# The last 512 tokens of a second layer by Strassen's seven products instead of eight

## The chip, the cores and the metric

The kernel runs on one core of a Trainium2 chip. The metric is the device time of one launch in microseconds, taken as the median of several runs. The engines are TensorE (PE, matmuls; PEld is its weight load), VectorE (DVE), ScalarE (ACT), GpSimd (POOL) and SyncE (SP), which only issues transfers. SBUF is the on-chip memory, PSUM the accumulators that TensorE writes.

## The reference

Eight batches of attention with RMS-normalised queries and keys (12 heads, 448 tokens, 64 channels) give 3584 tokens of 768 channels. They go through two layers with a tanh-GELU between:

```python
q_n, k_n = rmsnorm(q, g_q), rmsnorm(k, g_k)
attn = softmax(q_n @ k_n.T / sqrt(64))
x = (attn @ v) as (3584, 768)
h = x @ w_in                      # 768 -> 2048
g = gelu_tanh(h)
out = g @ w_out                   # 2048 -> 768, float32
```

## The kernel before

The work goes batch by batch. `attention(b)` computes the scores, exponentials and products of batch b, and between them TensorE runs the second layer of earlier batches, in steps whose order is a string written out by hand. Behind each attention comes the first layer of that batch (`mm1_turn`, line 537), whose result ScalarE passes through the GELU (line 543) into `g`.

`g` is one SBUF tile of 128 partitions, 16 slices f of d_ff, and 2 x 448 tokens: two batches side by side. `wout` holds the second layer's weights, 128 partitions, the same 16 slices f, and 768 columns. Both are bf16. A second-layer result for 128 tokens is a sum over the 16 slices f. Two batches make seven such token tiles. Those that `attention` takes are computed with 64 x 64 tiles of the array (`quartered`, line 495); the ones that are left after the last batch, tiles 3 to 6 of the last pair, 512 tokens, are computed by `final` with the full array (`whole`, line 463): for each token tile two halves of HD = 384 columns, each 16 matmuls. The last half of the last tile is cut in two pieces of 192 columns. Each piece is copied from PSUM to an SBUF tile `osb` by ScalarE (line 704) or VectorE (line 706) and stored by `store` (line 456), two transfers of 64 rows each. Those go to SP's queue; the last ones are shared between SP and ScalarE.

PSUM tiles come from `pair`, which hands out four tiles in turn (t_100, t_101, t_892 and t_893 in the program's names).

In the first layer of the last batch, eight GELUs each fill two slices f of `g` (896 elements per partition). The list `m1` holds functions that are issued at given steps f of that layer; for the last batch it is empty. The order on every engine is that of the code; a wait is put before an instruction for the regions that it reads and writes.

Other names: `kT` holds the transposed keys, `vb` two tiles of values, and tiles with tag `ex` hold exponentials; nothing reads them behind the last attention. `sqp` is a pool for squares of queries and keys.

Of the kernel before, what the change touches and what calls it, by code (L numbers as in the profile page):

```python
# [8 lines left out]
F32 = mybir.dt.float32  # L9
BF16 = mybir.dt.bfloat16  # L10
# [7 lines left out]
def kernel(  # L18
# [11 lines left out]
    nc = tc.nc  # L30
    B, H, S, D = q.shape
    assert (B, H, S, D) == (8, 12, 448, 64)
    d_model = H * D
# [4 lines left out]
    P = 128  # L38
    R = 64
    NT = S // R  # L40
    NCH = H // 4
    HP = H // 2
    nf = d_ff // 128
    HD = d_model // 2
# [6 lines left out]
    sqp = ctx.enter_context(tc.tile_pool(name="sqp", bufs=2))  # L51
# [4 lines left out]
    exq = ctx.enter_context(tc.tile_pool(name="exq", bufs=2))  # L56
    xp = ctx.enter_context(tc.tile_pool(name="xp", bufs=2))
    gp = ctx.enter_context(tc.tile_pool(name="gp", bufs=1))
    op = ctx.enter_context(tc.tile_pool(name="op", bufs=3))
# [3 lines left out]
    start = ctx.enter_context(ExitStack())  # L63
# [6 lines left out]
    def pair(name):  # L70
        rounds.append(rounds.pop(0))
        return rounds[-1]
# [35 lines left out]
    wout = wts.tile([128, nf, d_model], BF16)  # L108
    vb = [wts.tile([P, HP, NT, D], BF16, name=f"vb{i}") for i in range(2)]
    ones = consts.tile([P, D], BF16)  # L110

    kT = consts.tile([128, NCH, NT, 2, R], BF16)
    raws, sqs, sss, rinvs, nrms = {}, {}, {}, {}, {}
    qT, xT = {}, {}
    g = gp.tile([128, nf, 2 * S], BF16, tag="g", name="g")
# [54 lines left out]
    def total(b, c, n, hs=both, ts=slice(0, NT)):  # L170
        if b not in sss:
            sss[b] = smp.tile([P, NCH, 2, 2, NT], F32, tag="ss", name="ss")
        nc.vector.reduce_sum(  # L173
            sss[b][:, seat(b, c), "qk".index(n), hs, ts], squares(b, c, n, hs, ts), axis=AX.X
        )
# [44 lines left out]
    def rsqrt_newton(b):  # L220


        rinvs[b] = smp.tile([P, NCH, 2, 2, NT], F32, tag="rinv", name="rinv")
        cs, flat = slice(0, NCH - 1), "p c n a t -> p (c n a t)"
        y, ms = rinvs[b][:, cs].rearrange(flat), sss[b][:, cs].rearrange(flat)
        t = smp.tile([P, NCH * 4 * NT], F32, tag="lg", name="lg")[:, :(NCH - 1) * 4 * NT]
        nc.vector.tensor_scalar(ms, ms, 1.0 / D, 1e-6, op0=ALU.mult, op1=ALU.add)
        nc.vector.tensor_scalar(
            y.bitcast(I32), ms.bitcast(I32), -0.5, float(0x5F3759DF), op0=ALU.mult, op1=ALU.add
        )  # L230
        for i in range(3):
            nc.vector.tensor_mul(t, y, y)
            nc.vector.scalar_tensor_tensor(t, t, -0.5, ms, op0=ALU.mult, op1=ALU.mult)
            if i < 2:
                nc.vector.scalar_tensor_tensor(y, t, 1.5, y, op0=ALU.add, op1=ALU.mult)

        m = 2 * NT
        for js, dst in ((slice(m, None), y[:, m:]), (slice(0, m), place(b, 0)[:, :m])):
            nc.vector.scalar_tensor_tensor(
                dst, t[:, js], 1.5, y[:, js], op0=ALU.add, op1=ALU.mult  # L240
            )

    def rsqrt_last(b, c=slice(NCH - 1, NCH)):

        flat, m = "p c n a t -> p (c n a t)", (c.stop - c.start) * 4 * NT
        y, ms = rinvs[b][:, c].rearrange(flat), sss[b][:, c].rearrange(flat)
        dst, z, u = y, None, ms
        if not steady():
            z, u = oall[0][:, S:S + m], oall[0][:, S + m:S + 2 * m]
            dst = place(b, 1)  # L250
        t = smp.tile([P, NCH * 4 * NT], F32, tag="lg", name="lg")[:, :m]
        nc.vector.tensor_scalar(u, ms, 1.0 / D, 1e-6, op0=ALU.mult, op1=ALU.add)
        nc.vector.tensor_scalar(
            y.bitcast(I32), u.bitcast(I32), -0.5, float(0x5F3759DF), op0=ALU.mult, op1=ALU.add
        )
        for i in range(3):
            if z is not None:
                nc.vector.tensor_copy(z, y)
            half = t if z is None else z
            nc.vector.tensor_mul(t, y if z is None else z, y)  # L260
            nc.vector.scalar_tensor_tensor(half, t, -0.5, u, op0=ALU.mult, op1=ALU.mult)
            nc.vector.scalar_tensor_tensor(
                y if i < 2 else dst, half, 1.5, y, op0=ALU.add, op1=ALU.mult
            )
# [8 lines left out]
    def normed(b, c, n, eng, ts=slice(0, NT)):  # L273
        if (n, b, c) not in nrms:
            nrms[n, b, c] = nrmp.tile([P, NT, 2, D], BF16, tag=f"nrm{n}", name=f"nrm{n}")
        m = ts.stop - ts.start
        root = rinvs[b][:, seat(b, c), "qk".index(n)] if eng is nc.gpsimd else roots[n, b, c]
        eng.tensor_mul(  # L278
            nrms[n, b, c][:, ts].rearrange("p t a d -> p a t d"),
            raws[n, b, c][:, :, ts],  # L280
            root[:, :, ts].to_broadcast([P, 2, m, D]),
        )
# [28 lines left out]
    def trans(b, c, eng=nc.vector):  # L311
        for n in "qk":
            turn(b, c, n)
            put(b, c, n, eng=eng)
# [9 lines left out]
    def gain(b, c):  # L324
        nc.vector.tensor_scalar(kT[:, c], kT[:, c], gcol[:, 0:1], None, op0=ALU.mult)
# [121 lines left out]
    osbs = {}  # L447

    def osb_of(i):
        osbs[i] = op.tile([128, d_model], F32, tag="osb", name="osb")  # L450

    def store(b, i, lo=0, hi=d_model, engs=(nc.sync, nc.sync)):
        for j, eng in enumerate(engs):
            col = i * 128 + j * R
            r = ((b // 2) * 2 + col // S) * R
            eng.dma_start(
                out_v[col % S // R, r:r + R, lo:hi], osbs[i][j * R:(j + 1) * R, lo:hi]
            )

    def whole(i, o, lo, hi):  # L460

        for f in range(nf):
            nc.tensor.matmul(  # L463
                o, g[:, f, i * 128:(i + 1) * 128], wout[:, f, lo:hi],
                start=(f == 0), stop=(f == nf - 1),
            )
# [117 lines left out]
    def attention(b, side, extra, ends):  # L584
# [57 lines left out]
        def go_on():  # L642
            for queue, eng in ((vector, nc.vector), (scalar, nc.scalar), (vector, nc.vector)):
                while queue and made.issuperset(needs(*queue[0])):
                    run(*queue.pop(0), eng)
# [41 lines left out]
        made.add(("p", 1))  # L687
        go_on()

    def final(b):  # L690

        last = 2 * S // 128 - 1
        for i in range(last - 3, last + 1):
            osb_of(i)
            for half in range(2):
                parts = [(half * HD, (half + 1) * HD)]
                if half and i == last:
                    parts = [(HD, HD + HD // 2), (HD + HD // 2, d_model)]
                for lo, hi in parts:
                    po = pair("o")[:, 0, :hi - lo]  # L700
                    whole(i, po, lo, hi)
                    end = hi == d_model
                    if half == 0 or i == last and not end:
                        nc.scalar.copy(osbs[i][:, lo:hi], po)
                    else:
                        nc.vector.tensor_copy(osbs[i][:, lo:hi], po)  # L706
                    if i == last and half:
                        store(b, i, lo if end else 0, hi, (nc.sync, nc.scalar))
            if i < last:
                store(b, i)  # L710

    def first_attention(side, mid):

# [25 lines left out]
    def plan(*entries):  # L739
        steps = {}  # L740
        for slot, *fns in entries:
            steps.setdefault(slot, []).extend(fns)
        return steps
# [185 lines left out]
    def normed_both(b, c, eng):  # L929
        for n in "qk":  # L930
            normed(b, c, n, eng)

    for b in range(B):
        m1, side, extra, ends = [], [], [], []
        if b == 0:

            m1 = [(0, lambda: total(1, 0, "k"),
                   lambda: total(1, 2, "q"), lambda: total(1, 2, "k"),
                   lambda: rsqrt_newton(1), lambda: normed_both(1, 2, nc.gpsimd),
                   lambda: normed(1, 0, "k", nc.gpsimd)),  # L940
                  (2, lambda: total(1, 1, "q"), lambda: total(1, 1, "k"),
                   lambda: normed(1, 0, "q", nc.vector), lambda: rsqrt_last(1),
                   lambda: normed_both(1, 1, nc.vector)),
                  (6, lambda: trans(1, 0, nc.scalar)),
                  (7, lambda: trans(1, 1))]
# [45 lines left out]
                extra.append(("first", lambda n=n: total(b + 2, 2, n)))  # L991
        if 0 < b and b + 1 < B:
            extra.append(("first", lambda: gain(b + 1, 2)))
        m1 = plan(*m1)
        for f in range(nf // 2 if b == 0 else nf):
            i, part = f // 4 * 2, f % 4
# [24 lines left out]
        if b + 1 == B:  # L1021
            final(b)
            break
# [44 lines left out]
```

## Time and profile before

| what | value |
|---|---|
| runs | 390.85, 390.27, 390.86 us; median 390.85 |
| profiled execution | span 389.1 us from the first to the last instruction; the page gives no other time of it |
| TensorE busy | 381.8 us (98%) |
| VectorE busy | 242.0 us (62%) |
| ScalarE busy | 278.2 us (71%) |
| GpSimd busy | 126.1 us (32%) |
| granted TensorE clock | 1.000 |
| last first layer on TensorE | 346.31 to 364.47 us |
| last stage on TensorE | 364.47 to 385.43 us |

Times in the profile count from the start of the span. A group of instructions reads: line, engine, operation, output and inputs by name, partitions x elements and type, count, busy us, mean ns of one, and the idle time of the engine just before it with what ended it. Matmuls are pipelined, so the length of one is more than the step from one to the next. A few per cent of the matmul records can be missing.

### The profile page before, as it was taken

What the parts mean: (1) busy time and instruction counts of PE and PEld (TensorE: products, weight loads), DVE (VectorE), ACT (ScalarE), POOL (GpSimd) and SP (SyncE); (2) the same over time, 40 slices, a digit from 0 to 9 for tenths busy, and PEclk for the clock granted to TensorE, in tenths of its full rate; (3) what the DMA queues carried; (4) which work ended last, traced back from release to release, by engine and by line L of the source; (5) the groups of instructions that cost most, each with busy time, mean ns of one, the idle gap of its engine ahead of it and who ended that gap; (6) DMA issues with size and microseconds to landing.
All of it is one profiled execution on the core that took longest, in us unless ns stands there. A gap on an engine that the chain in (4) does not pass through costs nothing.

```text
span 389.1 us, 17513 instructions
## 1 busy us (share of the span) xinstructions
PE 381.8 (98%) x8044; PEld 296.3 (76%) x8044; DVE 242.0 (62%) x367; ACT 278.2 (71%) x351; POOL 126.1 (32%) x109
## 2 busy tenths in 40 slices
PE   8899999999999999999999999999999999999996
PEld 5465586679987788877888788877888778887664
DVE  5998939985896359836589257953688304980010
ACT  6995589777994689757995589946897449944300
POOL 5996504448005440093103740063400900000000
PEclk9999999999999999999999999999999999999999
DMA  7999999979914992269722995169622721120033
GB/s 258 326 232 210 210 222 239 260 175 192 209 44 106 256 197 60 76 154 257 133 64 65 189 253 103 47 115 241 110 68 61 121 48 42 44 65 4 2 81 83
DMA packets 64446, 54.68 MB, mean 141 GB/s; under 512 B 37620, under 2 KB 60020, under 8 KB 64372
## 3 DMA queue, kind: packets, MB, share of 16 engines
q1 hardware_dynamic: 53936, 41.33, 44.0%
q0 software_dynamic: 10128, 11.80, 18.3%
q8 instruction: 63, 1.03, 1.1%
q10 hardware_dynamic: 308, 0.43, 0.3%
q14 instruction: 11, 0.09, 0.1%
HBM read 45.61 MB, written 11.01 MB: 146 GB/s over the span
## 4 chain that ended last, share of the span: by engine, by line
PE 92%; ACT 4%; DMA 1%; POOL 1%; SPq 0%; DVE 0%; issue 0%; DVEq 0%
PE t L537 33%; PE t L495 32%; PE t L387 9%; PE t L335 7%; PE t L463 5%; PE t L556 4%; ACT ex L343 4%; DMA rawq<-in_q_dram 1%; POOL g L164 1%; PE h L436 1%; PE o L387 0%; PE tp L296 0%; SPq L750 0%; DVE ss L173 0%; PE os L387 0%
## 5 line engine op out<-in xcount | busy, mean ns | idle before, releaser
L343 ACT ACTIVATE ex<-t,shift 128x896 bf16<-128x896 f32 x168 | 156.2, 1012 | 2.6 <-PE t L335 2.1
L495 PE MATMUL t<-wout,g 64*64 64x384 bf16 (+1 forms) x3456 | 152.0, 305 | 0.0
L495 PEld LDWEIGHTS <-g 64*64 64x64 bf16 x3456 | 115.3, 107 | 17.7 <-issue 0.2
L537 PE MATMUL t<-xT,win 64*64 64x448 bf16 x2688 | 128.7, 349 | 0.0
L537 PEld LDWEIGHTS <-win 64*64 64x64 bf16 x2688 | 97.8, 107 | 29.4
L543 ACT ACTIVATE g<-t 128x896 bf16<-128x896 f32 x56 | 50.5, 915 | 56.8 <-PE t L537 56.7
L173 DVE TENSOR_REDUCE ss<-sq 128x14 f32<-128x896 f32 (+3 forms) x45 | 44.3, 999 | 48.7 <-ACT sq L162 46.4
L335 PE MATMUL t<-qT,kT 64*64 64x448 bf16 x672 | 59.7, 352 | 1.9 <-ACT ex L343 0.6
L800 POOL COPY mark<-es 1x1 bf16<-1x1 bf16 x7 | 1.2, 177 | 134.9 <-DVE es L362 126.6
L278 POOL TENSOR_TENSOR nrmq<-rawq,rinv 128x896 bf16<-128x896 f32 (+1 forms) x21 | 34.8, 1659 | 18.8 <-ACT rinv L205 8.4
L355 DVE TENSOR_TENSOR es<-ex 128x1792 bf16<-128x1792 bf16 x21 | 22.2, 1059 | 29.5 <-ACT ex L343 29.5
L278 POOL TENSOR_TENSOR nrmk<-rawk,rinv 128x896 bf16<-128x896 f32 (+1 forms) x21 | 34.6, 1647 | 0.0
L387 PE MATMUL t<-ex,vb 64*64 64x448 bf16 x588 | 32.4, 350 | 0.2 <-issue 0.2
L335 PEld LDWEIGHTS <-kT 64*64 64x64 bf16 x672 | 26.1, 106 | 8.1 <-DVE kT L305 2.0
L397 DVE STREAM_TRANSPOSE st<-t 128x448 f32<-128x448 f32 x42 | 24.8, 628 | 9.2 <-PE t L387 9.2
L387 PEld LDWEIGHTS <-vb 64*64 64x64 bf16 x672 | 23.2, 107 | 8.3 <-issue 1.8
L409 DVE STREAM_TRANSPOSE rb<-rc 128x896 f32<-128x896 f32 (+1 forms) x25 | 26.7, 1068 | 0.3
L706 DVE COPY osb<-t 128x384 f32<-128x384 f32 (+1 forms) x4 | 2.0, 508 | 35.2 <-PE t L463 35.2
L422 DVE TENSOR_TENSOR xT<-t,rb 128x896 bf16<-128x896 f32 x21 | 22.8, 1087 | 0.9
L513 ACT COPY osb<-t 128x768 f32<-128x768 f32 (+1 forms) x18 | 12.6, 700 | 14.0 <-PE t L495 14.0
L358 DVE TENSOR_TENSOR es<-es,ex 128x1792 bf16<-128x1792 bf16 x21 | 22.3, 1062 | 0.0
L164 POOL TENSOR_TENSOR sq<-rawq 128x896 f32<-128x896 f32 (+1 forms) x9 | 13.6, 1510 | 24.1 <-DVE ss L173 17.4
(102 smaller groups left out, 318.4 us busy)
## 6 DMA issues: line engine op xcount, KB each, us to landing
rawq<-in_q_dram SPq DMA_DIRECT2D x22, 448.0 KB, 5.0
rawk<-in_k_dram SPq DMA_DIRECT2D x22, 448.0 KB, 6.3
out_dram<-osb SPq DMA_DIRECT2D x42, 192.0 KB, 2.7
vb<-in_v_dram POOLq DMA_DIRECT2D x6, 672.0 KB, 7.6
win<-in_moe_w_in_dram POOLq DMA_DIRECT2D x8, 384.0 KB, 11.1
wout<-in_moe_w_out_dram POOLq DMA_DIRECT2D x3, 768.0 KB, 17.6
out_dram<-osb SPq DMA_DIRECT2D x24, 96.0 KB, 2.5
vb<-in_v_dram POOLq DMA_DIRECT2D x2, 448.0 KB, 16.2
```

What stands on the lines that cost most here:

```text
L173: nc.vector.reduce_sum(sss[b][:, seat(b, c), "qk".index(n), hs, ts], squares(b, c, n, hs, ts), axis=AX.X)
L278: eng.tensor_mul(nrms[n, b, c][:, ts].rearrange("p t a d -> p a t d"), raws[n, b, c][:, :, ts], root[:, :, ts].to_broadcast([P, 2, m, D]),)
L335: nc.tensor.matmul(sc[r * R:(r + 1) * R, a, :S], kT[rs, c, t, r], qT[b][rs, c, :, r], start=True, stop=True,)
L343: nc.scalar.activation(exs[b, c][:, t], scs.pop((b, c, t))[:, :, :S], AF.Exp, scale=scale, bias=shift)
L358: nc.vector.tensor_add(es, es, ex[:, 4:6])
L387: nc.tensor.matmul(o[r][a * D:(a + 1) * D], vb[b % 2][rs, 2 * c + a, i] if what else ones[rs], es[i][rs, a], start=(i == 0), stop=(i == n ...
L397: nc.vector.transpose(st[:, r].rearrange("p a b -> p (a b)"), o[r])
L409: nc.vector.transpose(oas["rb"][:, rs].rearrange("p r s -> p (r s)"), rc.to_broadcast([128, (rs.stop - rs.start) * m, 32]),)
L422: nc.vector.tensor_mul(xT[b][:, 2 * c:2 * c + 2], oas["o", c, 1][:, :, :S], oas["rb"])
L495: mm = nc.tensor.matmul(o[a * R:(a + 1) * R, bank, :hi - lo], g[rs, f, at:at + R], wout[rs, f, lo:hi], start=(n == 0), stop=(n == len(step ...
L537: mm = nc.tensor.matmul(h[a * R:(a + 1) * R, j, :S], win[rs, c, at:at + R], xT[b][rs, c], start=begin and c == cs[0], stop=end and c == cs ...
L543: nc.scalar.activation(g[:, 2 * i:2 * i + 2, (b % 2) * S:(b % 2 + 1) * S], h[:, :, :S], AF.Gelu_apprx_tanh,)
```

## The change

The 512 tokens are taken as two groups of 256 (A1 and A2), the 16 slices f as eight pairs, and the 768 columns as two halves. That makes each operand a 2 x 2 block matrix: A11 is the first group at the even slices, A12 at the odd ones, A21 and A22 the same for the second group; B11 and B12 are the column halves of `wout` at the even slices, B21 and B22 at the odd ones. Each of the eight block products of before is a sum over 8 slices; the changed `final` makes seven (Winograd's form of Strassen's method), each for two token tiles of 128.

Four sums of weight blocks and four of token blocks are needed first. VectorE makes them: `weight_sum` and `token_sums` are put into the list `m1` of the last first layer, and the last quarter of the token sums stands at the head of `final`. The sums go to tiles with tag `ex`, to `kT`, to both tiles of `vb`, and in place to `wout` (B12) and `g` (A21). Products 1 and 2 need no sums and come first. Every product but the first of each tile is evicted by a VectorE add of PSUM and an `osb` tile; product 5 is added twice. The stores are of half width (384 columns), and the last of 192.

```diff
+    def token_sums(js):
+        a11, a21 = g4[:, js, 0, late1], g4[:, js, 0, late2]
+        a12, a22 = g4[:, js, 1, late1], g4[:, js, 1, late2]
+        nc.vector.tensor_sub(sa[3][:, js], a21, a11)
+        nc.vector.tensor_add(sa[2][:, js], sa[3][:, js], a22)
+        nc.vector.tensor_add(a21, a21, a22)
+        nc.vector.tensor_sub(sa[4][:, js], a12, sa[2][:, js])
...
+    def weight_sum(i):
+        x, y = {3: (b12, b22), 2: (b11, sw[3]), 4: (b21, sw[2]), 1: (b12, b11)}[i]
+        nc.vector.tensor_sub(sw[i], x, y)
...
     def final(b):
-        for i in range(last - 3, last + 1):
...
-                    whole(i, po, lo, hi)
...
+        token_sums(slice(NJ - 2, NJ))
...
+        def product(i, t, lo=0, hi=HD):
+            o = pair("o")[:, 0, :hi - lo]
+            for j in range(NJ):
+                lhs, rhs = operands(i, j, t)
+                nc.tensor.matmul(o, lhs, rhs[:, lo:hi], start=(j == 0), stop=(j == NJ - 1))
+            return o
...
+        for t in range(2):
+            c1, c2 = tiles[t]
+            nc.scalar.copy(c2[:, first], product(1, t))
+            add(c1[:, first], product(2, t), c2[:, first])
+            put_out(t, 0, first)
+        for t in range(2):
+            c1, c2 = tiles[t]
+            add(c1[:, last], product(6, t), c2[:, first])
+            add(c2[:, first], product(7, t), c1[:, last])
+            p5 = product(5, t)
+            add(c2[:, last], p5, c2[:, first])
+            add(c1[:, last], p5, c1[:, last])
+            put_out(t, 1, last)
+            add(c2[:, first], product(4, t), c2[:, first])
+            put_out(t, 1, first)
+            if t == 0:
+                add(c1[:, last], product(3, t), c1[:, last])
+                put_out(t, 0, last)
+                continue
+            for lo in (0, HD // 2):
+                cols = slice(HD + lo, HD + lo + HD // 2)
+                add(c1[:, cols], product(3, t, lo, lo + HD // 2), c1[:, cols])
+                put_out(t, 0, cols, (nc.sync, nc.scalar))
...
+        if b + 1 == B:
+            m1.append((4, sums_homes))
+            m1 += [(f, lambda i=i: weight_sum(i)) for f, i in ((4, 3), (6, 2), (8, 4), (10, 1))]
+            m1 += [(f, lambda js=js: token_sums(js))
+                   for f, js in ((7, slice(0, 4)), (11, slice(4, 6)))]
```

Here NJ is 8, g4 and w4 are views of `g` and `wout` with the slices f as pairs, late1 and late2 are the two groups of 256 tokens, sw and sa are the sums, and c1 and c2 the `osb` tiles of the first and the second group. `operands` gives for products 1 and 2 blocks of `g` and `wout`, for 3 sa[4] and B22, for 4 A22 and sw[4], for 5, 6 and 7 a sum of each.

More of the change, by code (lines that the diff above doesn't have):

```diff
@@ L688, in attention @@
         go_on()
-    def final(b):
-        last = 2 * S // 128 - 1
-        for i in range(last - 3, last + 1):
[L694 to L700, printed above, removed]
-                    whole(i, po, lo, hi)
[L702 to L710, printed above, removed]
+    NJ = nf // 2
@@ new lines, with sums_homes, home @@
+    g4 = g.rearrange("p (j w) s -> p j w s", w=2)
+    w4 = wout.rearrange("p (j w) d -> p j w d", w=2)
+    TH = 2 * 128
+    late1, late2 = slice(2 * S - 2 * TH, 2 * S - TH), slice(2 * S - TH, 2 * S)
+    sw, sa = {}, {}
+    def sums_homes():
+        two = exq.tile([P, 2 * NJ, HD], BF16, tag="ex", name="tw")
+        one = exq.tile([P, NJ, HD], BF16, tag="ex", name="tw")
+        sw.update({3: two[:, :NJ], 2: two[:, NJ:], 4: one})
+        sw[1] = w4[:, :, 0, HD:]
+        def home(t):
+            return t[:, :NJ * TH].rearrange("p (j s) -> p j s", j=NJ)
+        sa[1] = g4[:, :, 0, late2]
+        sa[2] = home(kT.rearrange("p c t r s -> p (c t r s)"))
+        sa[3] = home(vb[0].rearrange("p h t d -> p (h t d)"))
+        sa[4] = home(vb[1].rearrange("p h t d -> p (h t d)"))
@@ new lines, in weight_sum @@
+    def weight_sum(i):
+        b11, b12 = w4[:, :, 0, :HD], w4[:, :, 0, HD:]
+        b21, b22 = w4[:, :, 1, :HD], w4[:, :, 1, HD:]
+        x, y = {3: (b12, b22), 2: (b11, sw[3]), 4: (b21, sw[2]), 1: (b12, b11)}[i]
[7 more added lines that the diff above has]
+        nc.vector.tensor_sub(sa[4][:, js], a12, sa[2][:, js])
@@ new lines, in final, with operands, put_out @@
+    def final(b):
+        token_sums(slice(NJ - 2, NJ))
+        tiles = [[op.tile([128, d_model], F32, tag="osb", name="osb") for _ in range(2)]]
+        tiles.append([
+            sqp.tile([P, 2, NT, D], F32, tag="sq", name="osb")
+            .rearrange("p a t d -> p (a t d)")[:, :d_model] for _ in range(2)
+        ])
+        first, last = slice(0, HD), slice(HD, d_model)
+        def operands(i, j, t):
+            lo = t * 128
+            if i in (1, 2):
+                a = g4[:, j, i - 1, late1.start + lo:late1.start + lo + 128]
+                return a, w4[:, j, i - 1, first]
+            if i == 4:
+                return g4[:, j, 1, late2.start + lo:late2.start + lo + 128], sw[4][:, j]
+            at, which, w = {
+                3: (sa[4], None, w4[:, j, 1, last]), 5: (sa[1], 1, None),
+                6: (sa[2], 2, None), 7: (sa[3], 3, None)}[i]
+            return at[:, j, lo:lo + 128], sw[which][:, j] if which else w
+        def product(i, t, lo=0, hi=HD):
[4 more added lines that the diff above has]
+            return o
+        def put_out(t, row, cols, engs=(nc.sync, nc.sync)):
+            i = 3 + 2 * row + t
+            osbs[i] = tiles[t][row]
+            store(b, i, cols.start, cols.stop, engs)
+        add = nc.vector.tensor_add
+        p4 = {}
+        for t in range(2):
[21 more added lines that the diff above has]
+                put_out(t, 0, cols, (nc.sync, nc.scalar))
```

## The prediction

> **What bounds the kernel now.** I read the page first, for the span and each engine's share:
>
> ```profile
> span 389.1 us, 17513 instructions
> PE 381.8 (98%) x8044; PEld 296.3 (76%) x8044; DVE 242.0 (62%) x367; ACT 278.2 (71%) x351; POOL 126.1 (32%) x109
> ```
>
> TensorE is busy for 98% of the span, so only less TensorE work, or a shorter tail behind it, can move the time. Next came the chain that ended last, in order of time (start, length, what):
>
> ```profile
> 346.31 18.16 PE t L537 x384
> 364.47 20.96 PE t L463 x144
> 385.43 0.03 DVEq L706
> 385.46 0.04 issue
> 385.50 0.36 DVE osb L706
> ```
>
> The last stage is one unbroken piece of TensorE, 364.47 to 385.43, with the last first layer (L537) straight before it and one VectorE copy behind it. Then the groups of that stage by shape (busy us, mean ns | idle before), and the timeline of ScalarE and VectorE (start, length):
>
> ```profile
> L463 PE MATMUL t<-wout,g 128*128 128x384 bf16 x104 | 17.1, 326 | 0.0
> L463 PE MATMUL t<-wout,g 128*128 128x192 bf16 x32 | 2.8, 247 | 0.0
> ```
> ```profile
> 347.51 1.09 DVE L422 TENSOR_TENSOR xT<-t,rb 128x896 bf16<-128x896 f32 x1
> 355.43 0.92 ACT L543 ACTIVATE g<-t 128x896 bf16<-128x896 f32 x1 [0.22 <-PE t L537]
> 359.97 0.92 ACT L543 ACTIVATE g<-t 128x896 bf16<-128x896 f32 x1 [0.22 <-PE t L537]
> 364.51 0.92 ACT L543 ACTIVATE g<-t 128x896 bf16<-128x896 f32 x1 [0.22 <-PE t L537]
> 367.25 0.48 ACT L704 COPY osb<-t 128x384 f32<-128x384 f32 x1 [1.82 <-PE t L463]
> 369.87 0.56 DVE L706 COPY osb<-t 128x384 f32<-128x384 f32 x1 [21.26 <-PE t L463]
> 382.85 0.48 ACT L704 COPY osb<-t 128x384 f32<-128x384 f32 x1 [4.72 <-PE t L463]
> 384.13 0.32 ACT L704 COPY osb<-t 128x192 f32<-128x192 f32 x1 [0.80 <-PE t L463]
> 385.50 0.36 DVE L706 COPY osb<-t 128x192 f32<-128x192 f32 x1 [4.74 <-PE t L463]
> ```
>
> The mean of 326 ns is a latency; the pace is in the copies. ScalarE's copies at 367.25 and 382.85 lie 96 matmuls of 384 columns apart: 15.60 / 96 = 0.1625 us each. Sixteen matmuls of 192 columns take 384.13 - 382.85 = 1.28 by one pair of copies and 1.37 by the other: 0.083 each. (The group shows 104 of 112 wide matmuls, since some records are missing; the code issues 112 and 32.) The other thing to see is the 21.26 us in which VectorE has nothing to do, from 348.60 on.
>
> **Part 1, the matmuls removed.** Seven products of 8 steps for each of two token tiles make 112 matmuls, of which 16 are half wide, in place of 112 wide and 32 half-wide ones. So 8 x 0.1625 + 16 x 0.083 = 1.30 + 1.33 = 2.63 us less on the path. The new ones have the same shape, and they load from kT, vb and the exp tiles as from g.
>
> **Part 2, the sums.** On VectorE, before and after (rows with their waits):
>
> ```order
> L422 TENSOR_TENSOR xT<-t_100,rb 128x896 [waits DVE_49,PE_49]
> L706 COPY osb<-t_892 128x384 [waits DMAHW2_49,DMAHW5_49,DMAHW1_49,DMAHW7_49,PE_49,Activation_49]
> L706 COPY osb<-t_100 128x384 [waits DMAHW3_49,DMAHW4_49,DMAHW0_49,DMAHW7_49,PE_49,Activation_49]
> L706 COPY osb<-t_892 128x384 [waits DMAHW6_49,DMAHW5_49,DMAHW7_49,DMAHW0_49,PE_49]
> L706 COPY osb<-t_893 128x192 [waits DMAHW0_49,DVE_49,DMAHW7_49,PE_49,Activation_49]
> ```
> ```order
> L422 TENSOR_TENSOR xT<-t_100,rb 128x896 [waits DVE_49,PE_49]
> L717 TENSOR_TENSOR tw<-wout 128x3072 [waits DMASW6_49,DMASW5_49,DMASW7_49,DMASW4_49,DMASW3_49]
> L717 TENSOR_TENSOR tw<-wout,tw 128x3072 [waits DVE_49]
> L723 TENSOR_TENSOR vb_121<-g 128x1024 [waits DMASW2_49,DMASW6_49,DMASW1_49,Activation_49]
> L724 TENSOR_TENSOR kT<-vb_121,g 128x1024 [waits DVE_49]
> L725 TENSOR_TENSOR g<-g 128x4x256
> L726 TENSOR_TENSOR vb_122<-g,kT 128x1024 [waits DVE_49]
> L717 TENSOR_TENSOR tw<-wout,tw 128x3072
> L717 TENSOR_TENSOR wout<-wout 128x8x384
> L723 TENSOR_TENSOR vb_121<-g 128x512 [waits Activation_49]
> ```
>
> Sixteen sums stand where VectorE was idle: four of 3072 elements, four of 1024, eight of 512 (the last four right behind row L723 and its three followers again). The rows for their price:
>
> ```profile
> L422 DVE TENSOR_TENSOR xT<-t,rb 128x896 bf16<-128x896 f32 x21 | 22.8, 1087 | 0.9
> L358 DVE TENSOR_TENSOR es<-es,ex 128x1792 bf16<-128x1792 bf16 x21 | 22.3, 1062 | 0.0
> L360 DVE TENSOR_TENSOR es<-es 128x896 bf16<-128x896 bf16 x20 | 12.5, 625 | 0.7
> L427 DVE TENSOR_TENSOR xT<-o,rb 128x448 bf16<-128x448 f32 x6 | 3.4, 613 | 0.2
> ```
> ```profile
> 341.37 1.05 DVE L358 TENSOR_TENSOR es<-es,ex 128x1792 bf16<-128x1792 bf16 x1
> 342.45 0.63 DVE L360 TENSOR_TENSOR es<-es 128x896 bf16<-128x896 bf16 x1
> 343.18 0.62 DVE L362 TENSOR_TENSOR es<-es,ex 128x896 bf16<-128x896 bf16 x1
> ```
>
> From bf16 in SBUF an element costs (1062 - 625) / 896 = 0.488 ns on a base of 188 ns; from f32 it is (1087 - 613) / 448 = 1.058 ns on 139 ns. A sum that follows another waits 0.03 to 0.10 us (the three dependent rows). The new sums are bf16 in SBUF, but their rows have gaps, which no row here shows; they are nearest to L358, which has the same operation, type and memory, so I take the cheap rate: 1.69, 0.69 and 0.44 us, plus 0.07 each. The dear rate (3.39, 1.22, 0.68) is the other end. The Trainium skill, "Advanced Engine Details and Errata", section VectorE Performance Modes, asks only for 16-bit data and a unit step in the innermost dimension for the two-per-cycle mode; by that the gaps cost nothing, and no row of this trace shows it.
>
> At the cheap rate: two weight sums 348.7 to 352.2; then VectorE waits for the fourth gelu pair (355.43 + 0.92 = 356.35); four token sums to 359.4; two weight sums to 362.9; four token sums to 364.9 (their gelus ended at 360.89); the last four wait for the last gelu (365.43) and end at 367.5. The first product that needs a sum starts after four that need none, at about 364.47 + 0.11 + 4 x 1.30 + 0.1 = 369.9, and asks for kT, the second of the last four, done at 366.5. That leaves 3.4 us, and 3.1 us for the next product's PSUM tile, which is free when VectorE has added the second product (368.1, needed 371.2). So the sums cost nothing; the cover is those four products. Another engine is not in their way: GpSimd does nothing in this stretch, and TensorE kept its pace where VectorE was busiest (busy us of each engine by stretch):
>
> ```profile
> 336.00:346.00 10.00, 10.00 (x303) 8.58 (x296) 9.06 (x14) 7.64 (x10) 0.00 (x0) 1.00 0.29 71
> 348.60:364.40 15.80, 15.80 (x337) 11.76 (x329) 0.00 (x1) 6.31 (x7) 0.00 (x0) 1.00 0.01 4
> ```
>
> **Part 3, the head of the stage.** TensorE before and after:
>
> ```order
> L463 LDWEIGHTS g
> L463 MATMUL t_893<-wout,g 128x384 [waits Activation_49]
> ...
> L463 LDWEIGHTS g [waits Activation_49]
> L463 MATMUL t_893<-wout,g 128x384
> L463 LDWEIGHTS g
> ```
> ```order
> L754 LDWEIGHTS g
> L754 MATMUL t_893<-wout,g 128x384 [waits Activation_49]
> ...
> L754 LDWEIGHTS g [waits Activation_49]
> L754 MATMUL t_893<-wout,g 128x384
> ...
> L754 LDWEIGHTS kT [waits DVE_49]
> L754 MATMUL t_893<-tw,kT 128x384 [waits Activation_49]
> ```
>
> The wait for the last gelu moves from the 15th matmul to the 8th, since product 1 takes every second f. It is due at 364.47 + 7 x 0.1625 = 365.61; the gelu ends at 365.43 and a weight load comes between. Bounds 0 and 0.25 us (gelu end plus the 0.10 of weight load seen in the LDWEIGHTS rows, plus a semaphore); I take 0.1. No wait for VectorE stands ahead of the first kT row, so in-place sums in g don't hold the first products.
>
> ```profile
> L463 PEld LDWEIGHTS <-g 128*128 128x128 bf16 x133 | 12.5, 98 | 6.7
> ```
>
> **Part 4, evictions and the tail.** Copies become adds with one PSUM operand. The nearest rows are the copy (558 ns at 384, 358 at 192) and a VectorE multiply from f32:
>
> ```profile
> L278 DVE TENSOR_TENSOR nrmk<-rawk,o 128x384 bf16<-128x384 f32 x2 | 1.1, 549 | 0.0
> ```
>
> I take 0.56 and 0.36. Each token tile has six or seven adds (3.4 us) over five products (6.5 us), so they keep up, and the last add is as long as the copy it replaces. What changes is SP's queue. Before and after, its last rows:
>
> ```order
> L456 DMA out_dram<-osb 64x768 [waits DMAHW3_49,DVE_49,Activation_49]
> L456 DMA out_dram<-osb 64x768 [waits DMAHW4_49]
> L456 DMA out_dram<-osb 64x576 [waits DMAHW6_49,Activation_49]
> L456 DMA out_dram<-osb 64x192 [waits DMAHW0_49,DVE_49]
> L1063 UNCONDITIONAL_BRANCH
> ```
> ```order
> L456 DMA out_dram<-osb 64x384 [waits DMAHW1_49,DVE_49]
> L456 DMA out_dram<-osb 64x384 [waits DMAHW2_49]
> L456 DMA out_dram<-osb 64x384 [waits DMAHW3_49,DVE_49]
> L456 DMA out_dram<-osb 64x384 [waits DMAHW5_49]
> L456 DMA out_dram<-osb 64x192 [waits DMAHW6_49,DVE_49]
> L456 DMA out_dram<-osb 64x192 [waits DMAHW0_49,DVE_49]
> ```
>
> Four more transfers stand right ahead of the last two, and each costs SP 466 ns (issue rows of SP in the last stage, min/median/max; then size and time to landing):
>
> ```profile
> L456 SPq DMA_DIRECT2D out_dram<-osb x8: 466/466/605, 370.5 to 385.9; - x8
> L456 ACTq DMA_DIRECT2D out_dram<-osb x2: 499/528/557, 384.5 to 385.9; - x2
> out_dram<-osb SPq DMA_DIRECT2D x6, 192.0 KB, 2.6
> out_dram<-osb SPq DMA_DIRECT2D x1, 48.0 KB, 1.9
> ```
>
> Count from the end of product 5 of the second tile, 0: adds end at 0.6 and 1.1; product 4 ends at 1.30 and its add at 1.9; SP issues its two stores 1.95 to 2.9; the first half of product 3 ends at 1.96, its add at 2.3, and its SP store waits until 2.9 and holds SP to 3.35; the second half ends at 2.63, its add at 3.06, and its store, which could go at 3.1, goes at 3.35. So about 0.3 us later than the copy-to-store step of before. Bounds: 0, if ScalarE's half landed last anyway, and 1.0, if the last transfer also takes the 2.6 us of a store in traffic and not 1.9. I take 0.3, nearest to the SP rows that set it. The Trainium skill's title page ("Trainium Kernel Development and Optimization", Key Constraints) says that issuing from several engines saves only the sequencer's issue time. That is the very thing short here: by that rule these 0.3 us would go if the stores were split over SP and ScalarE.
>
> **Sum.** -2.63 + 0 + 0.1 + 0.3 = -2.2 us: a span of 386.9. The median of before (390.85) stands 1.75 above the span shown, which is all that the page gives of the profiled execution; the same 1.75 gives 388.6.
>
> **Rivals.** A: VectorE runs the sums at the dear rate, for their row gaps. Then the weight sums end at 352.2 - 348.7 = 3.5 twice over: 355.6, the first four token sums at 361.5, weights at 368.4, the next token sums at 371.4, kT's last at 372.9 and all at 374.3. Product 6 stops at its seventh step (due 370.9) for 2.0 us; product 7 stops for its PSUM tile until the add behind the sums (374.9, due 373.3), 1.55 us. So 388.6 + 3.55 = 392.2, slower. It decides from the point at which the sums end 5.3 us late (3.1 of slack and 2.2 of gain); at the dear rate it is 6.8. For it: none of the bf16 rows shown has gaps. Against it: L358's rate. B: the tail is dearer, at its bound of 1.0 us: 389.3, still faster. For it: by the shapes in the order, 576 KB leave in the stores behind the last two PSUM tiles but one (four of 96 KB, four of 48), where it was 384 KB (two of 144, two of 48). Against it: the last store of before landed in 1.9 us behind 144 KB stores on the same two queues, and no store here is larger. C: the change doesn't get its products free: some wait at the head (a gelu or a PSUM tile) or a TensorE that slows while reading what VectorE just wrote gives back most of the 2.6: about 390.5, no change. The waits in the order and the window 336 to 346 speak against it.
>
> **How the numbers follow.** Forecast 388.6: 0.74. B: 0.11. A: 0.07. C: 0.05. Better than forecast (tail and head both at their lower bound, 388.2 or less): 0.03. What a measurement here can tell from no change is 0.2%, 0.8 us: under 390.07 is faster. Faster 0.74 + 0.11 + 0.03 = 0.88, within 0.05, slower 0.07. The range goes from 388.0 (no cost at head and tail, 388.2, and 0.2 for the runs' scatter of 0.6) to 389.7 (B plus 0.4 of that scatter).
>
> **What would show it.** Right: TensorE in the last stage about 18.3 us without a gap; the sums of 3072 elements at about 1.7 us and ended by 367.5; the last SP store starting some 0.3 us after the add before it. Wrong: a sum of 3 us, an idle stretch of TensorE at the first kT product, or a landing of the last store well past 2 us. What would make the number wrong without that is a tail whose landing depends on more than the issue.

## The result and the profile after

The changed kernel took 389.21 us (median of 4 runs, 389.0 to 389.53) beside 390.77 for the kernel before: a ratio of 0.9958, with a 95% interval of 0.9944 to 0.9972. It is faster, inside the range, but by 1.6 us and not by the 2.2 that was forecast; the time lies nearer to the 389.3 of rival B than to the forecast 388.6. The profiled execution took 389.53 us, with a span of 387.8; the spans of the four executions are 386.9, 387.2, 387.4 and 387.8.

First the page after, then the chain that ended last (start, length, what):

```profile
span 387.8 us, 17506 instructions
PE 379.0 (98%) x8020; PEld 294.2 (76%) x8020; DVE 259.9 (67%) x394; ACT 276.6 (71%) x348; POOL 126.0 (33%) x109
```
```profile
346.60 18.16 PE t L537 x384
364.76 18.34 PE t L754 x120
383.10 0.02 issue
383.13 0.36 DVE osb L785
```

The last stage on TensorE fell from 20.96 to 18.34 us, in one piece: all of the 2.62 us is there. But the span ends at 387.8, which is 387.8 - 383.49 = 4.31 us behind the end of the last add. Before, it was 389.1 - 385.86 = 3.24. So 1.07 us is given back behind the last arithmetic: 2.62 - 1.07 = 1.55, beside a measured gain of 1.56; with the scatter of these runs, an agreement that close is partly luck. (The profiled execution itself shows 0.29 less, since its last first layer began 0.29 later; that is treated below. Spans are given to 0.1 us, so such a difference is good to about 0.05.)

The sums on VectorE, in order of time:

```profile
348.81 1.75 DVE L717 TENSOR_TENSOR tw<-wout 128x3072 bf16<-128x3072 bf16 x1
350.59 1.76 DVE L717 TENSOR_TENSOR tw<-wout,tw 128x3072 bf16<-128x3072 bf16 x1
356.68 0.69 DVE L723 TENSOR_TENSOR vb<-g 128x1024 bf16<-128x1024 bf16 x1 [4.33 <-ACT g L543]
...
366.22 0.42 DVE L724 TENSOR_TENSOR kT<-vb,g 128x512 bf16<-128x512 bf16 x1
...
366.90 0.42 DVE L726 TENSOR_TENSOR vb<-g,kT 128x512 bf16<-128x512 bf16 x1
367.56 0.56 DVE L767 TENSOR_TENSOR osb<-t,osb 128x384 f32<-128x384 f32 x1 [0.25 <-issue]
```

They run at the cheap rate in spite of the gaps in their rows, and the last ends at 367.32. The trace agrees with the rule of the Trainium skill that the prediction named ("Advanced Engine Details and Errata", VectorE Performance Modes): 1.75 us for 3072 elements is 0.57 ns each, where the f32 rows of before had a slope of 1.058. (The section also asks for a start on a 4-byte boundary and for more than two elements; these operands have both.)

Now the stores. The issue rows of the end, two windows (count: min/median/max ns, first and last start us):

```profile
L456 SPq DMA_DIRECT2D out_dram<-osb x3: 467/588/760, 382.4 to 383.6; - x3
L456 ACTq DMA_DIRECT2D out_dram<-osb x2: 551/564/577, 382.9 to 383.5; - x2
...
L456 SPq DMA_DIRECT2D out_dram<-osb x2: 565/662/760, 383.6 to 384.4; - x2
...
DMA to landing us min/median/max: 1.9/2.0/2.2
```

The last add ends at 383.49, and ScalarE's store goes at once. SP's goes at 384.4, 0.9 us late. SP issued the two halves of the store ahead (the second group's first 384 columns) from 382.4 on (467 and 588 ns), then its half of the first piece of 192 columns at 383.6, beside ScalarE, in 760 ns. The landing of the last stores, 1.9 to 2.2 us, is as short as before.

### The profile page after: what moved, and what is told of

It reads as the page before. It is cut to its first block, busy times and chain, and to the rows that moved or that the text cites. A ratio compares the mean times of both kernels' runs of the same rounds, so it can differ in the third digit from the quotient of the medians.

```text
span 387.8 us, 17506 instructions
## 1 busy us (share of the span) xinstructions
PE 379.0 (98%) x8020; PEld 294.2 (76%) x8020; DVE 259.9 (67%) x394; ACT 276.6 (71%) x348; POOL 126.0 (33%) x109
## 4 chain that ended last, share of the span: by engine, by line
PE 92%; ACT 5%; DMA 1%; issue 1%; DVE 0%; POOL 0%
PE t L537 33%; PE t L495 32%; PE t L387 9%; PE t L335 8%; PE t L754 5%; ACT ex L343 4%; PE t L556 4%; DMA rawq<-in_q_dram 1%; PE h L436 1%; PE tp L296 1%; PE o L387 0%; POOL nrmq L278 0%; DVE ss L173 0%; ACT sq L162 0%; PE os L387 0%
## 5 line engine op out<-in xcount | busy, mean ns | idle before, releaser
L358 DVE TENSOR_TENSOR es<-es,ex 128x1792 bf16<-128x1792 bf16 x21 | 22.3, 1062 | 0.0
L325 DVE TENSOR_SCALAR kT<-kT,gcols 128x896 bf16<-128x896 bf16 x19 | 12.1, 639 | 11.2 <-DMA kT<-nrmk 11.2
```

## The experiments

Two readings stood against each other at first. Q: SP's queue of issues costs the missing part. E or B: the loss is in earlier stages, or in the bytes and their landing. In the kernel before, the time stood 1.72 to 1.94 us above the span in all 69 executions of the three chips below. In the kernels below whose last product comes in two pieces it stood more than 2.2 us above it in 28 of 82 executions, up to 3.4. That part of the time lies outside the span, and no trace here shows what it is spent on; so the median of the spans is given beside the time. The tail is the time from the end of the last add to the end of the span, in each profiled execution, good to about 0.05 us.

| kernel | time us | before us | ratio (95%) | median span us | tail us |
|---|---|---|---|---|---|
| changed, again | 390.10 | 390.57 | 0.9985 (0.9964 to 1.0007) | 387.35 | 5.66 |
| stores split | 388.22 | 390.57 | 0.9938 (0.9922 to 0.9954) | 386.1 | 3.37 |
| last stores all on SP | 390.76 | 390.57 | 1.0002 (0.9987 to 1.0017) | 388.7 | 5.32 |
| no sums | 389.87 | 390.57 | 0.9988 (0.9969 to 1.0007) | 387.8 | 4.29 |
| split, weight sums twice | 388.78 | 390.52 | 0.9949 (0.9928 to 0.9970) | 386.6 | 3.36 |
| split, all sums twice | 395.18 | 390.52 | 1.0117 (1.0069 to 1.0165) | 393.3 | 3.40 |
| split, last product whole | 388.55 | 390.52 | 0.9942 (0.9922 to 0.9962) | 386.75 | 3.44 |
| changed, third time | 389.26 | 390.52 | 0.9963 (0.9940 to 0.9985) | 387.3 | 4.25 |
| split, again | 388.50 | 390.60 | 0.9943 (0.9925 to 0.9961) | 386.5 | 3.43 |
| split, one store on GpSimd | 389.16 | 390.60 | 0.9951 (0.9934 to 0.9969) | 386.8 | 3.62 |

The kernel before had median spans of 388.8 (first four rows), 388.7 (next four) and 388.8 (last two); each group is one chip.

### The changed kernel again

No edit.

> The changed kernel once more, as it is, for the place of the missing 0.6 us. Theory Q (SP's queue): of the 2.62 us that TensorE saves, 1.07 is given back between the end of the last add and the end of the span, since the last SP store starts 0.9 us after the add that it waits for; the 0.3 us by which the last first layer began later in the profiled run (346.60 for 346.31) is scatter of one run. Then this run is again 389.2, its last SP store again starts 0.8 to 1.0 us late, and its last first layer begins at 346.0 to 346.7. Rival E (earlier stages): the new code delays something ahead of the last stage. Then the last first layer again begins 0.3 us or more late, behind a gap of TensorE near 256 to 301 us, and the stores are a smaller part.

Its last first layer began at 345.86, earlier than that of before; over all the profiled executions it began between 345.71 and 347.56, whatever the kernel. Rival E falls: the 0.29 us was scatter. The stores were late again, and worse:

```profile
364.02 18.34 PE t L754 x120
382.36 0.02 issue
382.38 0.36 DVE osb L785
```
```profile
L456 SPq DMA_DIRECT2D out_dram<-osb x4: 467/676/1725, 381.6 to 383.7; - x4
...
DMA to landing us min/median/max: 2.1/3.9/4.3
...
384.75:386.00 1.25, 0.00 (x0) 0.00 (x0) 0.00 (x0) 0.00 (x0) 0.00 (x0) 1.00 0.06 12
```

The add ends at 382.74, SP's last store goes at 383.7, takes 1.7 us to issue and lands late; the tail is 5.66. The last row (busy us of PE, PEld, DVE, ACT and POOL, granted clock, DMA share, GB/s) shows the DMA engines nearly still from 384.75 to 386.00, and the five stores that were issued from 382.1 on all landed late, 3.3 to 4.3 us after their issue. So in this execution the queue explains the 0.9 us by which the last store started late, as in the first one; the rest of the tail is landing, which is what rival B names, and it came in this profiled execution alone. The expected 389.2 was missed by 0.9 us, though the median span, 387.35, stands 1.45 under that of before, near the 1.56 by time of the first measurement. By time, this measurement does not tell the changed kernel from the kernel before: its interval reaches 1.0007. A fetch of instructions (queue q8) ran from 383.35 to 385.04 in this tail, and none in the first profile's; that it made the DMA engines stand still and the one issue take 1725 ns is not shown.

A third measurement, on the chip of the second group of rows, gave 389.26 us (389.2 to 390.1 expected), and its interval is below 1:

```profile
384.09 0.36 DVE osb L785
```
```profile
L456 SPq DMA_DIRECT2D out_dram<-osb x6: 467/571/758, 382.1 to 385.4; - x6
```

The add ends at 384.45, SP's last store goes at 385.4, again 0.9 us or more late, and the tail is 4.25.

### The stores split over two queues

```diff
+        tail = [(nc.sync, nc.sync), (nc.sync, nc.scalar)]
-            put_out(t, 1, last)
+            put_out(t, 1, last, tail[t])
-            put_out(t, 1, first)
+            put_out(t, 1, first, tail[t])
```

> Only the stores of the second token tile's lower row are moved: one half of each goes to ScalarE's queue instead of both to SP's. Theory Q: each queue then has 2 stores ahead of the last two at 0.47 to 0.59 us each, the last SP store starts within 0.15 us of its add, the tail from the last add's end falls from 4.3 to about 3.4 us, and the time from 389.2 to 388.3. Rival B (bytes and landing: the stores of 576 KB in the last 3 us are late whoever issues them): no change, 389.2, and a landing of the last store well over 2 us.

```profile
span 386.0 us, 17508 instructions
```
```profile
363.91 18.34 PE t L754 x120
382.25 0.02 issue
382.27 0.36 DVE osb L785
```
```profile
L456 SPq DMA_DIRECT2D out_dram<-osb x2: 547/552/556, 382.1 to 382.7; - x2
L456 ACTq DMA_DIRECT2D out_dram<-osb x2: 557/680/802, 382.1 to 383.0; - x2
```

The add ends at 382.63, SP's last store goes at 382.7, and the tail is 386.0 - 382.63 = 3.37. The same bytes become ready at the same steps, so rival B falls: it is the queue that issues them. The time is 388.22, as expected. ScalarE's own last store is now 0.4 us late, since its issue of the one ahead took 802 ns beside SP's. The run on a third chip gave 388.50:

> The split kernel once more, on another chip, as the reference for the next one and for the size of its gain. Theory Q: tail from the last add's end 3.3 to 3.4 us again, 388.2 to 388.6, that is 0.6% under the kernel before. If its earlier 388.2 was scatter: 389.2 and a tail over 4 us.

Its tail is 3.43. In both, the split kernel beats the kernel before by 0.6%; the changed one it beats by 1.25 us of median span on the first chip. On the second, where the third measurement of the changed kernel stands (387.3), the split kernel itself was not run; two variants of it with the same tail, the doubled weight sums (386.6) and the whole last product (386.75), are 0.7 and 0.55 below, where about 1 was expected. The tails differ by 0.8 to 0.9 us in the profiles with a normal landing (4.31 and 4.25 for 3.37 and 3.43).

### The last stores all on SP

```diff
-                put_out(t, 0, cols, (nc.sync, nc.scalar))
+                put_out(t, 0, cols, (nc.sync, nc.sync))
```

> The other direction: the two pieces of 192 columns go to SP's queue alone, so that SP has two more issues at 0.5 to 0.6 us behind the four that are ahead of them. Theory Q: last SP store 0.9 + 0.3 to 0.9 us behind its add (two issues more, less the 0.17 by which ScalarE's issuing at the same moment made one of them longer), time 389.7 to 390.1. Rival B (bytes and landing): 389.2, since the bytes and their times of readiness are the same.

```profile
382.52 0.36 DVE osb L785
```
```profile
L456 SPq DMA_DIRECT2D out_dram<-osb x6: 466/567/593, 381.8 to 384.9; - x6
...
DMA to landing us min/median/max: 1.9/2.0/2.2
```

The last store goes at 384.9, 2.0 us behind its add (382.88), and the tail is 5.32: 1.0 more than in the changed kernel's first profile. By time it is 0.7 us over the changed kernel beside it, by median span 1.35, and the gain of the change is gone. The delay came out above the expected 1.2 to 1.8, and the time above the expected 389.7 to 390.1. With SP alone no issue took 760 ns: in the profiles that length appears only where ScalarE issues too. That alone doesn't make it: before, SP and ScalarE issued their last stores together in 467 and 499 ns. What makes the long one is open.

### Without the sums

All sixteen sums left out; products 3 to 7 take plain blocks.

> The sixteen sums are left out: products 3 to 7 take plain blocks of wout and what g, kT and vb hold, so that the output is not the reference's. All matmuls, adds and stores stay. Theory (the sums are covered): 389.2, TensorE's last stage again 18.3 us. Rival S (the sums disturb TensorE or the GELUs, or the wait for the last ones costs at the head): 388.9 or less, with the last stage under 18.3 us or the last first layer under 18.16.

```profile
346.23 18.16 PE t L537 x384
364.39 18.34 PE t L751 x120
```

Both stages have the lengths that they have with the sums, and the tail is 4.29. Rival S expected 388.9 or less; 389.87 was measured (0.7 over the theory's 389.2 too), and the median span, 387.8, is not under the 387.35 of the changed kernel. The sums are covered.

### How far the cover reaches

Both kernels have the split stores. In the first, each weight sum is made a second time, with an extra line of this form:

```diff
         nc.vector.tensor_sub(sw[i], x, y)
+        x, y = {3: (b12, b22), 2: (b11, sw[3]), 4: (b21, sw[2]), 1: (b21, sw[2])}[i]
+        nc.vector.tensor_sub(sw[i if i > 1 else 4], x, y)
```

> On top of the split stores, each of the four weight sums is made twice (four sums of 3072 elements more, 7 us of VectorE; where the sum is made in place, another is repeated). Theory (the cover is the idle time of VectorE plus the four products without sums): two of the four go into the 4.3 us that VectorE waits for the fourth GELU pair; the other two push the last token sums from 367.3 to 369.6, kT's last to 368.9, which is due at 370.9. So nothing shows: 388.2, last stage 18.3 us. Rival S (VectorE's work beside TensorE has a price of its own, by SBUF or by waits): some part of 7 us shows, 388.7 or more.

```profile
356.33 0.69 DVE L725 TENSOR_TENSOR vb<-g 128x1024 bf16<-128x1024 bf16 x1 [0.74 <-ACT g L543]
...
368.27 0.42 DVE L728 TENSOR_TENSOR vb<-g,kT 128x512 bf16<-128x512 bf16 x1
368.61 0.55 DVE L769 TENSOR_TENSOR osb<-t,osb 128x384 f32<-128x384 f32 x1
```
```profile
364.42 18.34 PE t L756 x120
```

7 us more on VectorE, and TensorE's stage is still 18.34: the wait for the GELU shrank from 4.33 to 0.74, and the sums end at 368.69. The time, 388.78, is by its number what rival S asked for (388.7 or more), but its interval, 387.7 to 389.3 us, holds the split kernel's 388.22 and 388.50 too; what decides is the stage's length and the tail, 3.36. In the second kernel the token sums are doubled too (the sum in place stays single and another is made three times):

> On top of the split stores, all sums are made twice, which is the dear rate of rival A in the prediction without its cause. Theory: kT's last sum ends near 374.9 and all near 376.7; product 6 stalls 0.75 us at its fifth step and 3.2 us at its seventh, product 7 stalls 2.0 us for its PSUM tile: 6 us in all, 394.2, with the last stage at 24.3 us. Prediction's own figure for the dear rate: 3.55 us, 391.8. Rival (sums are free at any rate): 388.2.

TensorE in that stage, and windows of it (length, busy us of PE, PEld, DVE, ACT and POOL, then granted clock, DMA share, GB/s):

```profile
369.02 1.37 PE L759 MATMUL t<-tw,kT 128*128 128x384 bf16 x6
373.20 0.50 PE L759 MATMUL t<-tw,kT 128*128 128x384 bf16 x2 [2.81 <-DVE kT L728]
375.25 2.72 PE L759 MATMUL t<-tw,vb 128*128 128x384 bf16 x8 [1.55 <-DVE osb L772]
377.76 1.72 PE L759 MATMUL t<-wout,g 128*128 128x384 bf16 x8
379.32 0.98 PE L759 MATMUL t<-tw,g 128*128 128x384 bf16 x5
```
```profile
371.46:374.87 3.41, 0.50 (x2) 0.21 (x3) 3.24 (x9) 0.00 (x0) 0.00 (x0) 1.00 0.00 0
374.87:378.28 3.41, 3.03 (x10) 1.47 (x10) 1.53 (x4) 0.00 (x0) 0.00 (x0) 0.50 0.38 88
378.00:383.00 5.00, 5.00 (x31) 2.99 (x30) 2.69 (x5) 0.00 (x0) 0.00 (x0) 0.97 0.35 82
```

The stage grows by 6.4 us (24.74 for 18.34), close to the expected 6.0, and the two stalls stand where rival A of the prediction put them. The seventh step of product 6 starts at 373.20 instead of 370.00 (3.2 us); product 7 starts 1.73 us later than a step behind it; of the expected 0.75 at the fifth step 0.2 came. Then product 7 itself takes 2.51 us to the next product's start instead of 1.30, and the next one 1.56: 1.47 us more, under a granted clock that is 0.50 from 374.87 to 378.28. Here a VectorE that was late cost the wait and then a slower TensorE.

### Two tries at the rest of the tail

The second tile's product 3 in one piece of 384 columns:

```diff
-            for lo in (0, HD // 2):
+            add(c1[:, last], product(3, t), c1[:, last])
+            put_out(t, 0, last, tail[t])
```

> Split stores, and product 3 of the second tile in one piece of 384 columns, stored once on each queue. Theory Q: the last add is 0.2 us longer (0.56 for 0.36), but each queue issues one store less, so that ScalarE's last store no longer starts 0.35 us behind its add: within 0.2 us of the split kernel, 388.1. Rival (the landing of 96 KB in place of 48 KB sets the end): 388.7.

```profile
383.80 0.56 DVE osb L779
```
```profile
L456 SPq DMA_DIRECT2D out_dram<-osb x1: 467/467/467, 384.4 to 384.4; - x1
L456 ACTq DMA_DIRECT2D out_dram<-osb x1: 498/498/498, 384.4 to 384.4; - x1
...
DMA to landing us min/median/max: 2.2/2.3/2.4
```

Both stores go as the add ends (384.36), but they land in 2.2 to 2.4 us, and the tail is 3.44: the time is that of the split kernel within the interval, and lies between what Q (388.1) and the rival (388.7) expected. All its 12 executions stand as near to their span as those of before (1.73 to 1.85 us), which holds for no other changed kernel with as many; why is not shown. One half store on GpSimd's queue:

```diff
-                put_out(t, 0, cols, (nc.sync, nc.scalar))
+                put_out(t, 0, cols, (nc.sync, nc.scalar if lo else nc.gpsimd))
```

> Split stores, and one half of the last store but one goes to GpSimd's queue in place of ScalarE's. In the split kernel ScalarE's issue of that store took 0.80 us beside SP's, so that its last store started 0.35 us behind its add. Theory Q (the tail is the issue queues): ScalarE's last store starts at once, the tail falls from 3.4 to 3.1 us, 387.9 to 388.2. Rival: the store on GpSimd's queue lands later than the last ones do (GpSimd's loads here land 7 us and more after their issue), and the time is 0.3 us or more over the split kernel's.

```profile
L456 ACTq DMA_DIRECT2D out_dram<-osb x2: 497/498/499, 382.1 to 383.2; - x2
...
L456 POOL DMA_DIRECT2D out_dram<-osb x1: 599/599/599, 382.8 to 382.8; - x1
...
DMA to landing us min/median/max: 1.9/2.1/2.5
...
L1144 SPq EVENT_SEMAPHORE  x1: 28/28/28, 385.4 to 385.4; - x1
L1144 POOLq DRAIN  x1: 3205/3205/3205, 382.8 to 382.8; - x1
```

ScalarE's last store goes as its add ends (383.18), as Q expected, yet the tail is 3.62 instead of 3.4. The rival's reason is not what happened either: no store landed later than 2.5 us. (Its figure for the loads is too high as well: in this trace the two quickest loads on GpSimd's queue landed 3.7 and 6.6 us after their issue.) GpSimd issued its store 0.3 us behind its add (382.52), with a landing of 2.1, which is too early to hold the end. The last two rows show what does. They are closing steps of the program: SP's wait for its last store ends at 385.4, but GpSimd, now with a store of its own, stays in a DRAIN until 386.0, and only then do the last steps start. In the split kernel GpSimd's closing steps start at 385.3, right behind SP's last ones.

Nor did ScalarE's late store cost anything in the split kernel. There SP's eight closing waits run from 384.7, as its own last store lands, to 385.1, and ScalarE's store lands at 385.0, in time for the last of them. Of these kernels none is better than the split one beyond the noise.

## Why the prediction was right, and what it mis-sized

- **Part 1, the matmuls removed.** -2.63 forecast, -2.62 measured with the head in it. (The prediction's count is a slip of words: the stage has 120 matmuls, 104 wide and 16 half wide. Its sum, 8 wide and 16 half-wide ones fewer, is right.)
- **Part 2, the sums.** Right at the row chosen: 1.75, 0.69 and 0.42 us for 1.69, 0.69 and 0.44, and ended at 367.32 for 367.5. The run without sums shows no cost of theirs, neither in the two stages nor in the tail; the doubled weight sums show that the cover was real and larger than needed.
- **Part 3, the head.** 0.1 was forecast. Product 1's wait shows in TensorE's weight load (0.2 us in the waits), but the stage of 18.34 has no room for a cost on the path: 104 x 0.1625 + 16 x 0.083 = 18.23, and before there was the same rest of 0.1.
- **Part 4, the tail.** This term was mis-sized: 0.3 forecast, 1.07 measured, at the bound of 1.0 or just above it. SP's queue was named as the place, and the split stores show that it is. The step that failed is the price of an issue. I took 466 ns for each and nothing between them: three issues, 1.40 us. That price is the median of eight rows that mix first stores of a pair with second ones, though the same row shows 605 as the longest. In the changed kernel the pair costs 467 and 588, the next 760 beside ScalarE's issue, and the three steps from one to the next 0.24 us together: 2.05 us, so that SP is behind by 0.9 us and not by 0.3. The bound was argued from the landing, which did not move; it should have come from the longest issue. The remark that the 0.3 us would go if the stores were split was right in kind: the split took away 0.94 (4.31 to 3.37, each good to 0.05).
- **From span to time.** The same 1.75 us was added after as before. In the first measurement the four executions stood 1.73 to 2.10 us above their spans, which adds up to 0.35 us that the sum did not have; its cause is open.
- **Rivals.** A did not happen. The kernel with all sums doubled shows what it would have cost: its stalls are where A put them, but it cost 6.4 us for the 3.55 that A had: the stalls were 3.2 and 1.7 us for A's 2.0 and 1.55, and the slowed clock, which A did not have, added 1.5. B is the nearest to what happened, by its place and, with 1.0, nearly by its price, though not by its mechanism of landing. C did not happen: the stage has the 18.3 us that the removed matmuls leave.

## What to carry to other kernels

When arithmetic is cut in a last stage, the stores come closer together: count the issues on each queue behind the last products, at the price of the second and third issue in a row, and try them on two queues before anything else. Work put on an idle engine was free here as long as its last result was ahead of the first use; work that margin out from the waits that stand between, since a wait for an earlier producer absorbs extra work (here 3.6 of 7 us).

## What the runs showed of the hardware

- A store of 64 rows took SP 467 ns to issue when its queue was free and 546 to 605 right behind another. In the four profiles of the kernels with the changed kernel's stores, SP's third issue of the tail took 739 to 765 ns; in the four of kernels with the stores split, ScalarE's took 792 to 804 in that place. Both issue there at nearly the same moment, but elsewhere they do so at 467 and 499; ScalarE's others took 497 to 577. One issue took 1725 ns, with the DMA engines nearly still.
- VectorE sums of bf16 whose rows have gaps run at the rate of those without: 1750 ns for 3072 elements, also in place, where L358's rate gives 1690.
- A TensorE that stood for 2.81 us, and soon again for 1.55, ran the next eight matmuls at about half pace (2.51 us for 1.30), with a granted clock of 0.50 for 3.41 us (374.87 to 378.28). The Trainium skill, "TensorE: Matmul & The Clock Gate" (Part 1: The HAM clock gate), states a half-rate clock after an idle window of about 3.4 us; the trace agrees with the half rate, and here the 3.41 us ahead of it, with TensorE busy for 0.50 us of them and no single wait over 2.81, were idle enough.
- The program closes with waits on SP for the landings, about 0.06 us apart. In the split kernel a store on ScalarE's queue that landed 0.3 us behind SP's last one cost nothing, since its wait came last. In the kernel with one store on GpSimd's queue, GpSimd stood in a DRAIN of 3.2 us from that store's issue on, and the end came about 0.5 us later for it.
